# Early score tiles placed by the count of each row half, and first query rows and keys fetched earlier, in a fused attention and MLP kernel

## The chip, the cores and the metric

The kernel runs on one core of one Trainium2 chip. The time is device time in microseconds; the kernel before took 1616.31 us, the median of three runs (1616.12 to 1617.63). A core has a matrix engine (TensorE, called PE in the profile, with its weight loads as PEld), VectorE (DVE), ScalarE (ACT), GpSimd (POOL) and SyncE (SP), which here only issues DMA transfers. Matmul results go to PSUM, eight banks of 128 x 512 float32.

## The reference

For x of 2048 tokens by 512, a layer norm feeds an attention block of 32 heads of 16 and an MLP of width 1376; the output is x plus their product.

```python
xn = _layernorm(x, axis=-1)
s = _A_ref(xn, A_wqkv, A_wo)          # softmax(q k^T / 4) v, 32 heads, then @ wo
g = _silu(_B_ref(xn, B_w1, B_b1, B_w2, B_b2))   # gelu_tanh(xn @ w1 + b1) @ w2 + b2
return x + s * g
```

## The kernel before

**Stages.** The first stage (lines 382 to 520) normalizes x, transposes it and keeps it as a high part and a low part; every product of the projections is then three matmuls (high by high, high by low, low by high). It also computes the query and key rows of the first two head groups (`q_first`, four calls, one for each chunk of 512 tokens) and four of the value tiles (`v_tile`). Query and key rows are stored to device memory (`evac`, lines 373 and 374, queued on SP) and fetched again in another layout by `load_qs` (queries), `load_k` (keys) and `k_ones`.

The second stage, called the early stage here, runs the list `plan` (line 303): twelve value tiles in three `quad`s, 34 pairs of tiles of the MLP's first layer or of the remaining query and key rows (`half`, two for each pair), and 88 parts of the MLP's second layer (`down`). All its matmuls have a contraction of 64 rows. Two row tiles of the array are used, half 0 (rows 0 to 63) and half 1 (rows 64 to 127); `run` emits one matmul for each in turn, and one round of it is called a step here. There are 12 x (12 + 68) + 88 x 6 = 1488 steps, so 1488 of these matmuls (line 564) on each half.

The third stage is the attention itself: score tiles transposed, exponentials on ACT, products with the values (lines 712, 714, 778), then the output projection.

**The score tiles.** Before the exponentials can be taken, the maximum over keys of each query row and head has to be known. A score tile computes 128 query rows by 512 keys of one head with one matmul (line 180, contraction 48: high and low parts in three groups of 16 rows) and reduces it to two maxima on DVE (line 186). There are 32 units u (8 head groups by 4 chunks of queries) of 64 tiles. 4 x LEAD = 576 tiles, the units 0 to 8, are done in the early stage, between the other matmuls; the rest in the attention stage. Score tiles are done in turn on half 0 and half 1 (`made`), and their PSUM tiles come in turn from two banks, `ps_a` and `ps_b` (`s_ring`). When a unit is done, its maxima are negated and split (`s_end0`), which also asks for the query rows of the unit after next, and later transposed on PE (`s_end1`, line 260), copied by ACT (line 266) and stored.

**What places them.** `run` calls `fill(a)` ahead of each matmul of half a. `prog["n"]` counts the steps. `fill` emits a score tile if fewer have been made than `due`, which grows in a straight line from step FILL0 = 84 to step SLOTS = 1470, and if it is that half's turn; a transposition that has become ready takes the place of a tile.

**Waits between the halves.** A PSUM bank that was written from one half may be written from the other only after that; `mm` then has the matmul wait for a small ACT instruction (`mark`, line 577, tile `junk`), unless three later score tiles say that the earlier matmul is done (`taken`).

**Queues and errands.** SP issues its transfers in the order of the program. In the early stage `half` takes one entry each time from the list `errands`: the fetches of query rows (`ask_qs`) and of the keys of the next groups (`ask_k`: one for the rows of ones, six for the keys). The first query rows and keys are fetched at lines 716 to 718, behind the stores of the last `q_first`; the last call of the first stage, `v_tile(NCH - 1)`, stands at line 520. `load_k` fetches six pieces of 16 rows: three for each half.

**Order within a unit.** `at_of` turns a tile's number into a block of query rows and a chunk of keys; all units but u = 12 take the key chunks fastest.

Of the kernel before, what the change touches and what calls it, by code (L numbers as in the profile page):

```python
# [17 lines left out]
S = 2048  # L18
# [5 lines left out]
CH = 512  # L24
NCH = S // CH
# [7 lines left out]
LEAD = 144  # L33
NW = 10
EARLY = 4
DONE = 492
FILL0 = 84
HB = 4
W2B = 2
ORDER = {0: "TTTTV", 3: "TXSTTSTYV"}  # L40
# [1 line left out]
KB = 3  # L42
# [5 lines left out]
def fused(ctx: ExitStack, tc: tile.TileContext, x, wqk, wv, wo, w1, b1, w2, b2, out):  # L48
# [27 lines left out]
    def mm3(ps, lhs, rhs, first, last, then=None):  # L76
        n = 0
        for a, b in ((0, 0), (0, 1), (1, 0)):
            nc.tensor.matmul(ps, lhs[a], rhs[b], start=first and n == 0, stop=last and n == 2)  # L79
            n += 1  # L80
            if then:
                then()
# [14 lines left out]
    def rows(src, g, which, a, c0, n):  # L97
        r0 = g * P + 64 * which + DH * a
        return src[r0:r0 + 48, c0:c0 + n].rearrange("(p d) s -> d p s", d=DH)[:, 0:3:2, :]

    def load_k(g, pieces=range(6), eng=nc.sync, c0=0, n=S):
        both = kws[g % KB]
        for i in pieces:
            a, b = divmod(i, 3)
            r, cs = slice(64 * a + DH * b, 64 * a + DH * b + DH), slice(c0, c0 + n)
            src = rows((qk_h, qk_h, qk_l)[b], g, 1, a, c0, n)
            if both is not None:
                eng.dma_start(both[r, :, cs].bitcast(F32), src)
            else:
                for p in range(2):  # L110
                    eng.dma_start(kts[g % KB][p][r, cs].bitcast(F32), src[:, p])
# [16 lines left out]
    def q_rows(qs, u, sides=range(2)):  # L128
        g, c = divmod(u, NCH)
        for a in sides:  # L130
            for b, src in enumerate((qk_h, qk_l, qk_h)):
                r = 64 * a + DH * b
                nc.sync.dma_start(qs[r:r + DH].bitcast(F32), rows(src, g, 0, a, c * CH, CH))

    def load_qs(u, sides=range(2)):
        if u < NU:
            QS[u] = qzs[u % 2] if u < LEAD // 16 else qss[0][:, u % 2]
            q_rows(QS[u], u, sides)

    def ask_qs(u):  # L140
        for a in range(2):
            errands.append((load_qs, u, (a,)))

    def load_qt(u):
        QT[u] = qts[u % 2]
        q_rows(QT[u], u)
# [7 lines left out]
    made = [0, 0]  # L154
    done = {u: 0 for u in range(NU)}
    later, ended, errands, sent = [], [], [], set()

    def tick():
        for e in later:
            e[0] -= 1  # L160
# [7 lines left out]

    def at_of(job):
        u, st, p = job  # L170
        return divmod(st, NCH) if u != NCH * KB else divmod(st, NCH)[::-1]

    def s_mm(ps, job, a, c0, k0, w):
        u, st, p = job
# [20 lines left out]
    def s_whole(job, a):  # L195
        ps = s_tile()[0]
        s_mm(ps, job, a, 0, 0, CH)
        s_max(ps, job, a, slice(0, 2))

    def s_one(a):  # L200
        made[a] += 1
        s_whole(heads[made[a] - 1], a)
# [53 lines left out]
    prog = {}  # L256
# [23 lines left out]
    def w_new(src, bufs, tag):  # L280
        raw = wk.tile([P, CH], F32, name=tag, bufs=bufs)
        nc.sync.dma_start(raw, src)
        return raw
# [8 lines left out]
    VQ = 3  # L292
    first = [[("v", t // NCH, t % NCH) for t in range(i, i + 4)] for i in range(NT - 4 * VQ, NT, 4)]
    qs = [(2, 0), (2, 2)] + [(g, 0) for g in range(3, NG)] + [(g, 2) for g in range(3, NG)]
    nu, pairs = len(ms) // 2, []
# [8 lines left out]
    for j in range(len(pairs)):  # L304
        for h in range(2):
# [4 lines left out]
            due = next((i for i in range(j, len(pairs)) if is_m[i]), len(pairs))  # L310
# [4 lines left out]
            n = 2 if nd < len(parts) and parts[nd][2] and ready - nd > room else 1  # L315
            n = max(n, need - 2 * (left - 1))
# [27 lines left out]
    def w2_load(i):  # L344
        if i < len(ms):
            W2[ms[i][1:]] = w_new(w2[ms[i][2]], 2, "raw2")
# [31 lines left out]
    def v_out(t, pv):  # L378
        dst = vsb[:, t, :H * VW].rearrange("p (h w) -> p h w", w=VW)[:, :, :DH]
        nc.scalar.activation(dst, pv.rearrange("p (h w) -> p h w", w=DH), AF.Copy)  # L380

    with ExitStack() as s1:
# [4 lines left out]
        def a_tile(shape):  # L387
            banks[0] += 1
            i = banks[0] % 6
            if i < 3:  # L390
                return (ps_a, ps_b, ps_x)[i].tile(list(shape), F32, name="ps")
            return ps_t.tile(list(shape), F32, name="pst")
# [42 lines left out]
        def v_tile(t):  # L435
            pv = a_tile((P, D))
            c, ts = t // NCH, slice(t % NCH * P, t % NCH * P + P)
            for k in range(KT):
                mm3(pv, (xh[c][:, k, ts], xl[c][:, k, ts]), (wv_h[:, k], wv_l[:, k]), k == 0, k == KT - 1)
            v_out(t, pv)  # L440

        def q_first(c):
            pq = {}
            for g in range(2):
                ps = pq["q", g, c] = a_tile((P, CH))
                for k in range(KT):
                    ks = slice(k * P, (k + 1) * P)
                    mm3(ps, (W1[g][0][:, ks], W1[g][1][:, ks]), (xh[c][:, k], xl[c][:, k]), k == 0, k == KT - 1)
            evac(list(pq), pq)
# [58 lines left out]
        for c in range(1, NCH):  # L508
            for t in range(NCH * c, NCH * c + NCH):
                turn(t)  # L510
            if c < NCH - 1:
                ln(NCH * c + NCH, NCH)
            else:
                nc.scalar.activation(warm[:, 1:], warm[:, :1], AF.Gelu_apprx_tanh)
                w1_load(0)
                w2_load(0)
                w2_load(1)
            v_tile(c - 1)
            q_first(c)
        v_tile(NCH - 1)  # L520

    keep_r = ctx.enter_context(tc.tile_pool(name="keep_r", bufs=1, side="right"))
    qring = ctx.enter_context(tc.tile_pool(name="qring", bufs=2, side="right"))
# [6 lines left out]
    for i in range(2):  # L530
        qzs.append(qzp.tile([P, 2, CH], F32R, name=f"qz{i}"))

    prog.update(n=0, pe=0, seen=0)
    writer = {}
    s_when = []
    ndown = sum(1 for e in plan if e[0] == "down")
    SLOTS = 12 * (4 * VQ + 2 * len(pairs)) + 6 * ndown - 18

    def fill(a):
        due = 4 * LEAD * (prog["n"] - FILL0) // (SLOTS - FILL0)  # L540
        if sum(made) < min(due, 4 * LEAD) and (made[0] <= made[1]) == (a == 0):
            taken()
            if later and later[0][0] <= 0:
                u = later.pop(0)[1]
                s_end1(u)
                s_end2(u)
                return
            s_one(a)
            tick()

    def taken():
# [5 lines left out]
    def mm(a, key, ps, lhs, rhs, first, last):  # L557
        r = slice(64 * a, 64 * a + 64)
        token = None
        if not first and writer[key][0] != a and writer[key][1] > prog["seen"]:  # L560
            if not tokens or tokens[-1][0] < writer[key][1]:
                mark()
            prog["seen"], token = next(x for x in tokens if x[0] >= writer[key][1])
        i = nc.tensor.matmul(ps, lhs[r], rhs[r], start=first, stop=last).ins  # L564
        if token is not None:
            tc.add_manual_dep(i, token, SYNC, reason="other row tile")
        prog["pe"] += 1
        latest[0] = (prog["pe"], i.name)
        writer[key] = (a, prog["pe"])

# [104 lines left out]
    def quad(n):  # L675
        us = first[n]
        for u, b in zip(us, BANKS[n]):
            pool, name = {"x": (ps_x, "ps"), "m": (ps_m, "ps"), "v": (ps_v, "pv"), "t": (ps_t, "pst")}[b]
            PH[u] = pool.tile([P, CH], F32, name=name)
        for i in range(4):  # L680
            hooks = {6: [mark]} if i in (1, 2) else {}
            if n == VQ - 2 and i in (0, 2):
                hooks[3] = [lambda: w1_split(0) if i == 0 else w1_load(1)]
            run((terms(us[i], 0, i < 2), terms(us[(i + 2) % 4], 1, i < 2)), hooks)
            if i >= 2:
                for u in (us[i - 2], us[i]):
                    v_out(u[1] * NCH + u[2], PH.pop(u))
# [25 lines left out]
                         QT[u][r, p, :], start=True, stop=True)  # L713
        nc.scalar.activation(PT[u, k][:, 2 * p + a, :], ps, AF.Exp, scale=SCALE)  # L714

    load_k(0)
    load_qs(0)
    k_ones(kts[0])
    for n, e in enumerate(plan):
        if e[0] == "half":  # L720
            half(*e[1:])
        elif e[0] == "first":
            quad(e[1])
        else:
            if e[1] == parts[-2]:
                nc.scalar.activation(mhw, ident_r[:1, :1].bitcast(F32), AF.Exp)
            if e[1] == parts[-1]:
                for i in range(EARLY):
                    t_one(0, 0, i // 2, i % 2)
            down(*e[1])  # L730
        if e == ("first", VQ - 1):
            w2_split(0)
            w2_load(2)
            ask_qs(1)
            ask_k(1)
        if e[0] == "half" and pairs[e[1]][0] == ("q", NG - 1, 0) and e[2] == 1:
            kts.append([slot(p, (P, S), F32R) for p in range(2)])
            kws.append(None)
            qss.append(slot(2, (P, 2, 2, CH), F32R))
            ask_k(2)  # L740
        if n == len(plan) - 8:
            load_qt(0)
            load_mh(0)
# [172 lines left out]
    for t in range(NW):  # L916
        n = DONE + 2 * t
# [6 lines left out]
    for i, t in enumerate(late):  # L924
        n = L - 2 * len(late) - 1 + 2 * i
# [84 lines left out]
```

## Time and profile before

| | us |
|---|---|
| median of three runs | 1616.31 |
| profiled execution, its own time | 1617.43 |
| its span, first to last instruction | 1615.6 |
| PE busy | 1603.2 (99%) |
| DVE busy | 1388.1 (86%) |
| ACT busy | 1259.4 (78%) |
| POOL busy | 379.1 (23%) |
| early stage, first to last matmul of line 564 | 53.71 to 491.94 |

The span does not hold what lies ahead of the first instruction and behind the last; that is why the profiled execution's own time is 1.8 us more. A row of a timeline gives the start and the length in us, the engine, the line, the operation with output and inputs, the shape and how many instructions were merged into the row. A row of a stretch of time gives the length of the stretch, then busy time and instructions for each engine, the granted clock (1.00 is full speed), the busy share of the DMA engines and the GB/s they moved. The mean granted clock of the core was 0.999.

### The profile page before, as it was taken

The page shows a single profiled execution, that of the slowest core. Times are in us where ns is not written, and L with a number is a line of the kernel's source. Part 1 is how long each engine was busy: PE and PEld are TensorE (multiplying, and loading weights), DVE is VectorE, ACT ScalarE, POOL GpSimd, SP SyncE. Part 2 cuts the span into 40 slices and gives each one's busy share as a digit, 9 for nine tenths or more (in the row PEclk, how much of TensorE's full clock was granted, in tenths as well). Part 3 has the DMA queues.
Part 4 walks back from the last instruction along what each step waited for, and adds up shares of the span by engine and source line. Part 5 has one row for each costly group of instructions (what it writes and reads, how often), then busy time and mean ns, then how long its engine had stood idle before and what let it go on. Part 6 is the DMA issues. An engine that isn't in the chain of part 4 may idle for free.

```text
span 1615.6 us, 32457 instructions
## 1 busy us (share of the span) xinstructions
PE 1603.2 (99%) x12146; PEld 926.5 (57%) x12146; DVE 1388.1 (86%) x2267; ACT 1259.4 (78%) x2524; POOL 379.1 (23%) x398
## 2 busy tenths in 40 slices
PE   8999999999999999999999999999999999999998
PEld 7899999989995444444444444444444444444445
DVE  7299999989998999999999999999999999999733
ACT  4324333333338999999999999999999999999984
POOL 4235565655641001001100200000010000000144
PEclk9999999999999999999999999999999999999999
DMA  6615343453422113111511311231041111110152
GB/s 202 143 55 156 116 135 96 128 153 113 135 81 74 30 40 67 32 35 27 85 35 32 67 31 40 45 55 28 21 78 29 32 28 32 39 29 22 58 197 92
DMA packets 76223, 116.93 MB, mean 72 GB/s; under 512 B 24965, under 2 KB 26245, under 8 KB 74697
## 3 DMA queue, kind: packets, MB, share of 16 engines
q1 hardware_dynamic: 72604, 102.42, 23.3%
q0 software_dynamic: 3264, 12.35, 3.9%
q8 instruction: 96, 1.57, 0.4%
q14 instruction: 63, 0.51, 0.1%
q10 hardware_dynamic: 196, 0.07, 0.0%
HBM read 84.35 MB, written 25.97 MB: 68 GB/s over the span
## 4 chain that ended last, share of the span: by engine, by line
PE 97%; DVE 1%; ACT 0%; DMA 0%; issue 0%; SPq 0%; DVEq 0%; ACTq 0%
PE pv L778 32%; PE ps L180 18%; PE pst L712 15%; PE ps L564 13%; PE pst L564 7%; PE ps L712 5%; PE ps L79 3%; PE pv L564 2%; PE pst L79 1%; DVE slot L74 0%; DMA xt<-in_x 0%; ACT hh L367 0%; PE pst L260 0%; DVE st L408 0%; DVE xn L422 0%
## 5 line engine op out<-in xcount | busy, mean ns | idle before, releaser
L186 DVE TENSOR_REDUCE mx<-ps 128x2 f32<-128x512 f32 x2048 | 1307.8, 686 | 155.0 <-PE ps L180 97.6
L714 ACT ACTIVATE slot<-pst 128x512 f32<-128x512 f32 x1533 | 836.1, 614 | 14.5 <-PE pst L712 4.3
L778 PE MATMUL pv<-slot,vsb 128*32 128x512 f32 x4096 | 545.3, 605 | 0.0
L180 PE MATMUL ps<-kt,slot 48*128 48x512 f32 (+1 forms) x1364 | 393.3, 376 | 0.0
L712 PE MATMUL pst<-qt,kt 50*128 50x512 f32 x1149 | 378.7, 430 | 0.4 <-DVE gt L645 0.3
L714 ACT ACTIVATE slot<-ps 128x512 f32<-128x512 f32 x515 | 315.7, 614 | 14.0 <-PE pst L712 9.5
L712 PEld LDWEIGHTS pst<-qt,kt 50*128 50x128 f32 x1149 | 183.1, 184 | 248.3 <-ACT slot L714 245.1
L564 PE MATMUL ps<-slot,w1h 64*128 64x512 f32 x1088 | 232.9, 393 | 0.4 <-ACT junk L577 0.4
L180 PEld LDWEIGHTS ps<-kt,slot 48*128 48x128 f32 x1364 | 211.3, 184 | 34.6 <-DVE mx L186 23.4
L180 PE MATMUL ps<-kt,qz 48*128 48x512 f32 x512 | 218.8, 429 | 0.9 <-ACT mh L266 0.9
L180 PE MATMUL ps<-slot,slot 48*128 48x512 f32 (+1 forms) x598 | 172.5, 376 | 0.7 <-DVE mx L186 0.7
L564 PEld LDWEIGHTS ps<-slot,w1h 64*128 64x128 f32 x1088 | 159.9, 185 | 9.3 <-ACT junk L577 1.9
L712 PE MATMUL ps<-qt,kt 50*128 50x512 f32 x387 | 163.1, 423 | 0.0
L564 PE MATMUL ps<-slot,w1l 64*128 64x512 f32 x544 | 158.9, 393 | 0.0
L778 PEld LDWEIGHTS pv<-slot,vsb 128*32 128x32 f32 x4096 | 80.6, 108 | 119.5 <-issue 111.7
L368 POOL TENSOR_TENSOR hl<-hg,hh 128x512 fp32r<-128x512 f32 x76 | 96.7, 1294 | 133.6 <-ACT hh L367 83.6
L577 ACT ACTIVATE junk<-ident_r 1x1 f32<-1x1 f32 x92 | 18.1, 196 | 136.9 <-PE pst L564 133.0
L712 PE MATMUL pst<-qt,slot 50*128 50x512 f32 x384 | 119.7, 424 | 0.0
L712 PEld LDWEIGHTS ps<-qt,kt 50*128 50x128 f32 x387 | 71.2, 184 | 70.3 <-ACT slot L714 57.4
L712 PEld LDWEIGHTS pst<-qt,slot 50*128 50x128 f32 x384 | 61.5, 184 | 71.9 <-ACT slot L714 71.6
L180 PEld LDWEIGHTS ps<-slot,slot 48*128 48x128 f32 x598 | 92.6, 184 | 16.9 <-DVE mx L186 13.3
L244 POOL CAST nmh<-nm 128x16 fp32r<-128x16 f32 x32 | 6.3, 197 | 409.3 <-PE pst L712 258.0
(150 smaller groups left out, 1760.3 us busy)
## 6 DMA issues: line engine op xcount, KB each, us to landing
raw<-in_w SPq DMA_DIRECT2D x88, 256.0 KB
qk_h<-hh SPq DMA_DIRECT2D x32, 256.0 KB
qk_l<-hl SPq DMA_DIRECT2D x32, 256.0 KB
qt<-qk_h SPq DMA_DIRECT2D x128, 64.0 KB
slot<-qk_h SPq DMA_DIRECT2D x92, 64.0 KB
xt<-in_x SPq DMA_DIRECT2D x16, 256.0 KB
g_d<-gt POOLq DMA_DIRECT2D x16, 256.0 KB, 3.6
qt<-qk_l SPq DMA_DIRECT2D x64, 64.0 KB
```

The lines of the kernel that those rows point to most:

```text
L79: nc.tensor.matmul(ps, lhs[a], rhs[b], start=first and n == 0, stop=last and n == 2)
L180: return nc.tensor.matmul(ps[:, c0:c0 + w], QS[u][r, p, qi * P:(qi + 1) * P], kts[u // NCH % KB][p][r, k0:k0 + w], start=True, stop=True).ins
L186: nc.vector.tensor_reduce(MX[u][:, 2 * p:2 * p + 2, qi, ki][:, heads, parts], ps.rearrange("p (n c) -> p n c", c=HC), axis=AX.X, op=OP.max)
L244: nc.gpsimd.tensor_copy(hl[:, 0], nm)
L368: nc.gpsimd.tensor_sub(hl, raw, hh.bitcast(F32))
L564: i = nc.tensor.matmul(ps, lhs[r], rhs[r], start=first, stop=last).ins
L577: i = nc.scalar.activation(junk[:, :1], ident_r[:1, :1].bitcast(F32), AF.Copy).ins
L712: nc.tensor.matmul(ps, kts[g % KB][p][r, k * P:(k + 1) * P], QT[u][r, p, :], start=True, stop=True)
L714: nc.scalar.activation(PT[u, k][:, 2 * p + a, :], ps, AF.Exp, scale=SCALE)
L778: nc.tensor.matmul(PV[u][32 * j:32 * j + 32, :], vsb[:, k, h:h + 32], PT[u, k][:, j, :], start=(k == 0), stop=(k == NT - 1))
```

## The change

Score tiles are placed by a count of each half's own matmuls, `row[a]`, which takes in the score tiles. Tile number m goes to half a as soon as `row[a]` reaches FILL0 + m x ROWS / 576, with FILL0 = 38 and ROWS = 960 + 528 - 10 + 288 - 16 - 38 = 1712; `put` moves the due counts by two for each transposition that was emitted. The number of tiles stays 576.

The first stage's last part (`v_tile(NCH - 2)`, the last `q_first`, `v_tile(NCH - 1)`) is emitted after the pools of the next stage are opened; the query rows of unit 0 and the keys of its group, without the last 512 columns, are fetched ahead of it, and the last 512 columns behind it. The units 0, 12 and 24 now take the query blocks fastest, so that unit 0 begins with the first chunk of keys. Query rows asked for go to the front of the errands, and those of unit 1 are asked for after the first quad instead of the third.

```diff
-FILL0 = 84
+FILL0 = 38
@@
     def ask_qs(u):
-        for a in range(2):
-            errands.append((load_qs, u, (a,)))
+        errands[:0] = [(load_qs, u, (a,)) for a in range(2)]
@@
     def at_of(job):
         u, st, p = job
-        return divmod(st, NCH) if u != NCH * KB else divmod(st, NCH)[::-1]
+        return divmod(st, NCH) if u % (NCH * KB) else divmod(st, NCH)[::-1]
@@
                 w1_load(0)
                 w2_load(0)
                 w2_load(1)
+                break
             v_tile(c - 1)
             q_first(c)
-        v_tile(NCH - 1)
@@
         qzs.append(qzp.tile([P, 2, CH], F32R, name=f"qz{i}"))
 
+    load_qs(0)
+    load_k(0, c0=0, n=S - CH)
+    v_tile(NCH - 2)
+    q_first(NCH - 1)
+    v_tile(NCH - 1)
+    load_k(0, c0=S - CH, n=CH)
+
     prog.update(n=0, pe=0, seen=0)
     writer = {}
-    s_when = []
+    s_when, put, row = [], [0], [0, 0]
     ndown = sum(1 for e in plan if e[0] == "down")
-    SLOTS = 12 * (4 * VQ + 2 * len(pairs)) + 6 * ndown - 18
+    ROWS = 12 * (4 * VQ + 2 * len(pairs)) + 6 * ndown - 10 + 2 * LEAD - 2 * (LEAD // 16 - 1) - FILL0
 
     def fill(a):
-        due = 4 * LEAD * (prog["n"] - FILL0) // (SLOTS - FILL0)
-        if sum(made) < min(due, 4 * LEAD) and (made[0] <= made[1]) == (a == 0):
+        due = FILL0 + put[0] + sum(made) * ROWS // (4 * LEAD)
+        if sum(made) < 4 * LEAD and row[a] >= due and (made[0] <= made[1]) == (a == 0):
             taken()
             if later and later[0][0] <= 0:
+                put[0] += 2
                 u = later.pop(0)[1]
                 s_end1(u)
                 s_end2(u)
                 return
             s_one(a)
+            row[a] += 1
             tick()
@@
         prog["pe"] += 1
+        row[a] += 1
         latest[0] = (prog["pe"], i.name)
@@
-    load_k(0)
-    load_qs(0)
     k_ones(kts[0])
     for n, e in enumerate(plan):
@@
             quad(e[1])
+            if e[1] == 0:
+                ask_qs(1)
@@
             w2_load(2)
-            ask_qs(1)
             ask_k(1)
```

## The prediction

> **What bounds the kernel now.** I read the page's busy times and the chain of waits first, then the early stage by lines in one long stretch.
>
> ```profile
> PE 1603.2 (99%) x12146; PEld 926.5 (57%) x12146; DVE 1388.1 (86%) x2267; ACT 1259.4 (78%) x2524; POOL 379.1 (23%) x398
> PE 97%; DVE 1%; ACT 0%; DMA 0%; issue 0%; SPq 0%; DVEq 0%; ACTq 0%
> ...
> 64.97 2.75 PE ps L564 x24
> ...
> 73.50:487.00 413.50, 411.41 (x2768) 364.14 (x2766) 1.00 0.39 114
> ...
> 73.50:487.00 413.50, 245.51 (x575) 105.09 (x575) 1.00 0.39 114
> ```
>
> The third row is from the chain, the fourth and fifth are one stretch with the instructions of L564 and of L180 alone. PE sets the end, so what the early stage loses is lost at the end. Each matmul there uses one half of the array's rows, and two run at once: 24 matmuls in 2.75 us are 12 on each half, 0.229 us a place (I call a half's n-th matmul its place n). In the stretch with score tiles 2768 + 575 = 3343 matmuls took 413.5 us, or 0.247 us a place. PE shows as busy all the same, because one matmul's record is 0.39 us long and covers pauses. So pauses must be sought between starts. The stretch holds 575 score tiles, one every 0.719 us.
>
> The timeline of PE shows where the stage begins and ends, and how the halves run:
>
> ```profile
> 53.71 0.49 PE L564 MATMUL pst<-kt,slot 64*128 64x512 f32 x1
> ...
> 73.50 0.39 PE L180 MATMUL ps<-kt,qz 48*128 48x512 f32 x1
> 73.52 0.84 PE L564 MATMUL pst<-kt,slot 64*128 64x512 f32 x4
> 73.97 0.39 PE L180 MATMUL ps<-kt,qz 48*128 48x512 f32 x1
> ...
> 487.00 0.50 PE L180 MATMUL ps<-slot,qz 48*128 48x512 f32 x1
> ...
> 491.94 0.39 PE L564 MATMUL pst<-w2h,hl 64*128 64x512 f32 x1
> ```
>
> From the rule in fill, worked by hand: the first score tile stands at step 87, place 86 of half 0 (86 x 0.229 = 19.7 us after 53.71: 73.4, seen 73.50), the second at step 89, place 88 of half 1. In the order of the code five matmuls lie between them, three on half 0; yet they start 0.47 us apart, two places. So each half runs down its own list, and places, not steps, are time. In steps the tiles are 2 or 3 apart; a tile on half 1 follows by that many places, the next on half 0 by one more, its own half holding one more score tile. Counted out over 575 gaps: 270 gaps of three places, 172 of two, 117 of four, 16 others. Stretches of it, score tiles alone:
>
> ```profile
> 91.69 0.39 PE L180 MATMUL ps<-kt,qz 48*128 48x512 f32 x1
> ...
> 95.11 0.44 PE L180 MATMUL ps<-kt,qz 48*128 48x512 f32 x1
> ...
> 100.17 0.40 PE L180 MATMUL ps<-kt,qz 48*128 48x512 f32 x1
> 100.68 0.50 PE L180 MATMUL ps<-kt,qz 48*128 48x512 f32 x1
> 101.56 0.40 PE L180 MATMUL ps<-kt,qz 48*128 48x512 f32 x1
> 102.20 0.40 PE L180 MATMUL ps<-kt,qz 48*128 48x512 f32 x1
> 102.95 0.46 PE L180 MATMUL ps<-kt,qz 48*128 48x512 f32 x1
> 103.59 0.43 PE L180 MATMUL ps<-kt,qz 48*128 48x512 f32 x1
> ...
> 107.23 0.40 PE L180 MATMUL ps<-kt,qz 48*128 48x512 f32 x1
> ```
>
> Compare ends (start plus length). From 91.69 to 95.11, and from 100.17 to 103.59, five gaps of three places: 3.47 and 3.45 us for 15 places, 0.231 and 0.230 us each. From 103.59 to 107.23, gaps of 2, 4, 2, 4, 2: 3.61 us for 14 places, 0.258. So threes cost nearly what matmuls alone cost, and the uneven set loses 3.61 - 14 x 0.232 = 0.36 us.
>
> Why: two PSUM banks, each freed by a reduction on DVE.
>
> ```profile
> 100.60 0.69 DVE L186 TENSOR_REDUCE mx<-ps 128x2 f32<-128x512 f32 x1
> ...
> 101.21 0.69 DVE L186 TENSOR_REDUCE mx<-ps 128x2 f32<-128x512 f32 x1
> ...
> 102.78 0.68 DVE L186 TENSOR_REDUCE mx<-ps 128x2 f32<-128x512 f32 x1
> ...
> 100.67 0.18 PEld L180 LDWEIGHTS ps<-kt,qz 48*128 48x128 f32 x1
> ...
> 101.96 0.18 PEld L180 LDWEIGHTS ps<-kt,qz 48*128 48x128 f32 x1
> ```
>
> The load at 100.67 leads to the matmul ending at 101.18 (0.51 us); its reduction starts at 101.21 (0.03), ends at 101.90 (0.69), and the next load into that bank starts at 101.96 (0.06). At best a bank therefore serves a tile every 0.51 + 0.03 + 0.69 + 0.06 = 1.29 us. This particular bank took 102.78 - 101.21 = 1.57 us, because its load went ahead of a matmul still running and its reduction waited behind the other bank's. Reductions start no closer than 0.61 us (100.60, 101.21). A gap of two places (0.46 us) undercuts that, and two gaps of five places in all (1.16 us) undercut the bank; six places (1.39 us) do not.
>
> **The change part by part, and the sum.** No matmul, reduction or transfer of bytes is added or removed; 576 tiles stay in the stage.
>
> Spacing. The new rule counts places: 1712/576 = 2.972 per tile from place 38 on. Worked out the same way: 551 gaps of three places, 16 of two, 8 of five (where a transposition of the maxima stands between); first tile at place 38, last at 1763 (before: 86 and 1756, of 1776). Now 1725 places lie in the stretch instead of 1670.
>
> Other pauses, which both kernels have:
>
> ```profile
> 126.87 0.50 PE L180 MATMUL ps<-kt,qz 48*128 48x512 f32 x1
> ...
> 129.68 0.49 PE L180 MATMUL ps<-kt,qz 48*128 48x512 f32 x1
> ...
> 80.44 0.50 PE L564 MATMUL ps<-slot,w1h 64*128 64x512 f32 x1 [0.36 <-ACT junk L577]
> ...
> 360.10 0.50 PE L180 MATMUL ps<-kt,qz 48*128 48x512 f32 x1 [0.86 <-ACT mh L266]
> ```
>
> Between the first two rows stand ten places and one transposition: 2.80 - 2.32 = 0.48 us, eight times is 3.8. The two single waits are 0.36 + 0.86 = 1.2. The account of before: 1670 x 0.232 = 387.4, plus 3.8, 1.2 and some 58 uneven sets (575 gaps, ten to a cycle) x 0.36 = 20.9, is 413.3, against 413.5 measured.
>
> The new stage: 38 x 0.229 = 8.7; 1725 x 0.232 = 400.2; transpositions 3.8; single waits 1.2; sixteen two-place gaps between threes, which before does not show. Their price is at least 1.29 - 1.16 = 0.13 us and at most the 0.36 of a whole uneven set; I take 0.36, the nearer row being the whole set: 5.8. Tail: the 20 places behind the last tile took 491.94 - 487.00 + 0.23 = 5.2; seven fewer make it 3.6. With 0.5 for the first fetch, below, that is 423.8. Before: 19.8 + 413.5 + 5.2 = 438.5. The stage gets **14.7 us shorter**. The ends of the place price (0.229 to 0.2335) move this by -5.2 and +2.6, those of the gap by -3.7 and 0.
>
> First rows fetched earlier. Six loads of query rows and six of keys (three quarters of the columns) pass, on SP's queue, the four last stores and then go out; six small loads of the last quarter of the keys are new, 12 issues become 18.
>
> ```profile
> 45.08 1.92 SPq L282 DMA_DIRECT2D raw<-in_w  x4
> ...
> 55.43 0.79 SPq L108 DMA_DIRECT2D kt<-qk_h  x2
> ...
> 70.96 0.84 SPq L282 DMA_DIRECT2D raw<-in_w  x2
> ...
> 58.00:62.00 4.00, 1.00 1.03 164
> 62.00:66.00 4.00, 1.00 1.05 157
> ...
> 50.00:52.00 2.00, 1.00 0.43 162
> ```
>
> SP is free at 47.0 instead of 55.4, and the engines work off the weights by about 51 (busy share 0.43 in 50 to 52). The query rows (0.39 MB) and three quarters of the keys (1.18 MB) at 160 GB/s, the rate of the two stretches that carried keys, take 9.8 us: an estimate of 61. The new first tile stands at 53.71 + 8.7 = 62.4, and its partner on the other half, which needs the last of these pieces, at 63.1. The cover is 2 us, so the price is 0 to 2 us; I take 0.5, as completion comes after the last byte. Before, there was ample cover: the first tile stood at 73.5. The four stores behind these loads may go out some us late; behind them wait the last quarter (first read at tile 48, 53.71 + (38 + 48 x 2.97) x 0.23 = 95), the rows of ones and the weights of 70.96, whose place in the program does not move. If SP came late to those by more than a few us, ACT's split and the matmuls on it would wait the difference.
>
> Fetches of later query rows go to the front of the list of errands and the first of them is asked a hundred steps earlier: steps 105 and 111 for a tile at step 197. The keys of group 1 still finish at step 339, needed at 677; those of group 2 at 1089 instead of 1053, needed at 1318. Cost nothing; PE would stand still if one were late. The changed order of tiles for u = 24 touches the same tiles. Waits that hand a PSUM bank between halves fall from 12 to 9 by the same count, too few to enter.
>
> The profiled execution took 1617.43 with a span of 1615.6; the median of the runs is 1616.31. The attention stage follows unchanged, so 14.7 less is 1602.7 profiled and **1601.6 us** for the median.
>
> **The rivals.** (1) *The banks go on setting the pace.* If a tile still takes 0.719 us, the stretch stays at 413.5 but starts 11.1 us earlier and ends closer to the end: 8.7 + 413.5 + 3.6 + 0.5 = 426.3, or 12.2 less, 1604.1. For it: loads start right behind the freeing reduction. Against: the 0.230 of threes. The Trainium skill, page "TensorEngine Tiling (Array Packing)", section "PSUM Bottleneck", leans this way: tiling speeds up TensorE but not the evacuation of PSUM; the 1.29 us of a bank against 1.39 demanded says that here there is just room.
>
> (2) *The first tile waits for all keys*, as if the tile were one unit to its readers. Then the four stores and the last quarter come first: 3.0 MB at 160 GB/s from 51 is 69.8, 7.4 us after 62.4; 0.5 was in the sum: 1608.5. Against: the keys come in pieces with ranges of columns.
>
> (3) *The halves do not run apart.* If matmuls started strictly in the order of the code, seven matmuls would lie between tiles one way and three the other, four places and two. Each second reduction would wait 0.61 - 0.46 = 0.15 us, a bank would take 1.29 + 0.15 = 1.44 against 1.39 in demand: 287 pairs x 0.05 = 14 us, nearly all of the gain, 1616. Against: the 0.47 us above. The Trainium skill, page "TensorE: Matmul & The Clock Gate", section "The mechanism", does state strict program order for matmuls; this trace, with 0.47 us where that needs 0.69, disagrees for the two halves.
>
> (4) *Slower: the tiles lock in pairs.* If half 1 lags half 0 by more than 0.09 us, even threes come closer than 0.61 us in one direction, the late bank takes the 1.57 us seen above each time, and nothing breaks the beat since no gap of four comes to reset it. Then a tile costs 0.785, the stretch 575 x 0.785 + 5.0 = 456.4, the stage 469.2, 30.7 longer: 1647. It decides from (438.5 - 8.7 - 3.6 - 0.5)/575 = 0.740 us a tile on. For it: the ends in the second run of threes come 0.61 to 0.64 and 0.78 to 0.81 apart in turn. Against: their sum stays at 0.230 a place.
>
> **How the numbers follow.** My forecast holds with 0.62, rival 1 with 0.17, 2 with 0.07, 3 with 0.04, 4 with 0.08; 0.02 is left for something else that is slower. The range 1594 to 1609 has the ends of the two prices (1601.6 - 8.9 = 1592.7 if both fall out low together, so 1594), rival 1, and rival 2 at its top; 3, 4 and the rest lie outside. About 0.2%, 3.2 us, is what a measurement here can tell from no change. Faster: 0.62 + 0.17 + 0.07 = 0.86; within: 0.04; slower: 0.10.
>
> **What would show it.** First score tile at 62.4 (62 to 64; 70 for rival 2); the mean of 575 gaps 0.70 (0.72 rival 1, over 0.74 rival 4), with gaps of about 0.70 each way if 3 is wrong; loads no longer always 0.06 behind a reduction; the last matmul of L564 at 477; from there to the end as long as before. I am wrong if that last stage grows, or if the early gaps come out as before with no earlier first tile.

## The result, and the profile after

The changed kernel took 1607.73 us in the median (1606.84 to 1608.24, four runs) against 1616.21 (1615.77 to 1617.63, four runs) of the kernel before: a ratio of 0.9945, 95% interval 0.9928 to 0.9963. That is 8.5 us less, where 14.7 were forecast. The line numbers of the new kernel are one less up to the new code and 8 or 9 more behind it: score matmul L179 (was L180), reduction L185 (L186), the early stage's other matmuls L572 (L564).

The page's busy times and chain by engine:

```profile
PE 1594.5 (99%) x12146; PEld 915.4 (57%) x12146; DVE 1384.3 (86%) x2267; ACT 1261.6 (79%) x2525; POOL 377.6 (24%) x398
...
PE 98%; DVE 1%; DMA 0%; issue 0%; ACT 0%; SPq 0%; DVEq 0%; ACTq 0%
```

PE sets the end as before, with the same number of matmuls and 8.7 us less busy time, pauses between starts included. Where in the stage that lies shows in three stretches: from the first L572 matmul to the first score tile, from there to the last score tile, and to the last L572 matmul. The rows are those of score instructions alone (L179).

```profile
53.43:62.24 8.81, 0.00 (x1) 0.18 (x1) 1.00 0.97 134
62.24:479.62 417.38, 241.14 (x575) 105.13 (x575) 1.00 0.40 118
479.62:482.88 3.26, 0.40 (x1) 0.09 (x1) 1.00 0.42 155
```

| | before | after | difference |
|---|---|---|---|
| first other matmul to first score tile | 19.8 | 8.8 | -11.0 |
| first to last score tile | 413.5 | 417.4 | +3.9 |
| last score tile to last other matmul | 4.9 | 3.3 | -1.7 |
| from there to the end of the span | 1123.7 | 1123.6 | -0.1 |

All of the gain comes from the earlier start and the later last tile. The stretch with tiles did not keep its pace of 0.719 us a tile: 417.38/575 = 0.726. The attention stage has not moved by more than 0.1 us.

The start in PE's timeline, and SP's queue ahead of it:

```profile
62.24 0.39 PE L179 MATMUL ps<-kt,qz 48*128 48x512 f32 x1
62.25 1.07 PE L572 MATMUL pst<-kt,slot 64*128 64x512 f32 x5
63.62 0.47 PE L179 MATMUL ps<-kt,qz 48*128 48x512 f32 x1 [0.30 <-issue]
```

```profile
46.69 0.33 SPq L133 DMA_DIRECT2D qz<-qk_h  x1
...
55.08 0.41 SPq L108 DMA_DIRECT2D kt<-qk_l  x1
55.61 0.86 SPq L372 DMA_DIRECT2D qk_h<-hh  x1
...
70.30 0.83 SPq L281 DMA_DIRECT2D raw<-in_w  x2
```

The loads begin at 46.7; the last of the first three quarters of the keys is issued at 55.1, the first of the last stores at 55.6, and the next weights still at 70.3 (before: 70.96). The first tile starts at 62.24. Its partner on half 1, two places on, starts 1.38 us behind it; in e2 below, where the rows have long been there, it starts 0.47 behind. So the price of the fetch is 0.9 us at this tile.

Now a piece of the steady part. All gaps here are of three places.

```profile
91.09 0.39 PE L179 MATMUL ps<-kt,qz 48*128 48x512 f32 x1
91.22 0.39 PE L572 MATMUL pst<-kt,slot 64*128 64x512 f32 x1
...
91.69 0.39 PE L179 MATMUL ps<-kt,qz 48*128 48x512 f32 x1
...
92.48 0.45 PE L179 MATMUL ps<-kt,qz 48*128 48x512 f32 x1
92.62 0.39 PE L572 MATMUL pst<-kt,slot 64*128 64x512 f32 x1
...
93.09 0.43 PE L179 MATMUL ps<-kt,qz 48*128 48x512 f32 x1
93.94 0.39 PE L179 MATMUL ps<-kt,qz 48*128 48x512 f32 x1
94.53 0.40 PE L179 MATMUL ps<-kt,qz 48*128 48x512 f32 x1
```

```profile
91.68 0.69 DVE L185 TENSOR_REDUCE mx<-ps 128x2 f32<-128x512 f32 x1 [0.28 <-PE pst L572]
...
92.29 0.68 DVE L185 TENSOR_REDUCE mx<-ps 128x2 f32<-128x512 f32 x1
...
93.09 0.69 DVE L185 TENSOR_REDUCE mx<-ps 128x2 f32<-128x512 f32 x1
```

The tile of half 1 that starts at 91.09 ends at 91.48. Its reduction could follow 0.04 us behind, as others do; DVE is idle. It starts at 91.68, and the profile names an L572 matmul as what released it. That is the one of 91.22, which ends at 91.61, 0.07 before. In the code it stands ahead of the score tile; by the order of the code it is on half 0, whose list at that point holds one score tile more, so it runs a place later. The same at 92.48 (ends 92.93; the matmul of 92.62 ends at 93.01; the reduction starts at 93.09). The tile of half 0 that follows then finds DVE busy: from 91.68 to 92.29 is 0.61, the least distance of two reductions. So half 1's tile is late by a wait and half 0's by a queue, both hold their banks longer, and tiles end 0.60 and 0.80 to 0.85 us apart in turn: ends 91.48, 92.08, 92.93, 93.52, 94.33, 94.93. Over the whole stretch 258 of 287 reductions of half 1 start this way, on average 0.17 us behind their own tile, and 279 of 287 of half 0 start on DVE's heels, 0.18 us behind theirs. From one reduction to the next but one, the cycle of a bank, the median is 1.42 us; before, it was 1.40.

The list of waits shows the same, cut to reductions and to the stretch with tiles, with us, times and the longest; the first fence is the kernel before, the second the changed one:

```profile
DVE mx L186 <- PE ps L564: 8.2, 30, 0.7
DVE mx L186 <- PE pst L564: 4.4, 17, 0.3
...
DVE mx L186 <- PE pv L564: 2.1, 8, 0.3
```

```profile
DVE mx L185 <- PE ps L572: 8.4, 41, 0.7
DVE mx L185 <- PE pst L572: 5.1, 23, 0.7
DVE mx L185 <- PE pv L572: 1.8, 9, 0.3
```

A reduction takes its input from a score matmul alone, yet 55 times before and 73 times after it was another matmul that let an idle DVE go on. The list counts only idle times above 0.15 us, so these are fewer than the 258 above.

### The profile page after: what moved, and what is told of

It reads as the page before. It is cut to its first block, busy times and chain, and to the rows that moved or that the text cites. A ratio compares the mean times of both kernels' runs of the same rounds, so it can differ in the third digit from the quotient of the medians.

```text
span 1606.5 us, 32467 instructions
## 1 busy us (share of the span) xinstructions
PE 1594.5 (99%) x12146; PEld 915.4 (57%) x12146; DVE 1384.3 (86%) x2267; ACT 1261.6 (79%) x2525; POOL 377.6 (24%) x398
## 3 DMA queue, kind: packets, MB, share of 16 engines
q8 instruction: 96, 1.57, 0.4%
## 4 chain that ended last, share of the span: by engine, by line
PE 98%; DVE 1%; DMA 0%; issue 0%; ACT 0%; SPq 0%; DVEq 0%; ACTq 0%
PE pv L786 32%; PE ps L179 18%; PE pst L721 16%; PE ps L572 12%; PE pst L572 7%; PE ps L721 5%; PE ps L79 4%; PE pv L572 2%; PE pst L79 1%; DVE slot L74 0%; DMA xt<-in_x 0%; DVE st L407 0%; PE pst L259 0%; PE ps L259 0%; DVE xn L421 0%
## 5 line engine op out<-in xcount | busy, mean ns | idle before, releaser
L185 DVE TENSOR_REDUCE mx<-ps 128x2 f32<-128x512 f32 x2048 | 1300.2, 685 | 155.2 <-PE ps L179 86.1
L179 PE MATMUL ps<-kt,slot 48*128 48x512 f32 (+1 forms) x1364 | 393.1, 376 | 0.0
L179 PEld LDWEIGHTS ps<-kt,slot 48*128 48x128 f32 x1364 | 211.4, 184 | 34.5 <-DVE mx L185 25.6
L572 PE MATMUL ps<-slot,w1h 64*128 64x512 f32 x1088 | 220.1, 394 | 0.4 <-ACT junk L586 0.4
L179 PE MATMUL ps<-kt,qz 48*128 48x512 f32 x512 | 214.9, 420 | 0.3 <-issue 0.3
L179 PE MATMUL ps<-slot,slot 48*128 48x512 f32 (+1 forms) x598 | 172.4, 376 | 0.7 <-DVE mx L185 0.7
L572 PEld LDWEIGHTS ps<-slot,w1h 64*128 64x128 f32 x1088 | 152.5, 185 | 8.0 <-ACT junk L586 1.8
L572 PE MATMUL ps<-slot,w1l 64*128 64x512 f32 x544 | 143.0, 393 | 0.0
L179 PEld LDWEIGHTS ps<-kt,qz 48*128 48x128 f32 x512 | 93.7, 183 | 17.4 <-DMA kt<-qk_h 0.7
```

What stands on the lines that cost most here:

```text
L179: return nc.tensor.matmul(ps[:, c0:c0 + w], QS[u][r, p, qi * P:(qi + 1) * P], kts[u // NCH % KB][p][r, k0:k0 + w], start=True, stop=True).ins
L185: nc.vector.tensor_reduce(MX[u][:, 2 * p:2 * p + 2, qi, ki][:, heads, parts], ps.rearrange("p (n c) -> p n c", c=HC), axis=AX.X, op=OP.max)
```

## The experiments

Theory A, from these rows: a reduction waits for a count of finished matmuls in the order of the code. Rival B: the bank's pace comes from loads, reductions and PE alone. Rival C: PE itself is slower per place when score tiles are among its matmuls, whatever the banks do. All ratios are against the kernel before, run on the same chip.

**e1, tiles emitted first.** In the step, both halves' `fill` come ahead of both matmuls.

```diff
             for a in range(2):
                 fill(a)
+            for a in range(2):
                 mm(a, *two[a])
```

> The changed kernel, but in each step both halves' score tiles are emitted ahead of both other matmuls; places as in the changed kernel (threes). In its trace 258 of 287 reductions of half 1 start 0.07 us behind the end of an L572 matmul that ends later than their own score tile. Theory A: a reduction waits for a count of finished matmuls in the order of the code, so a tile of half 1, emitted behind its step's matmul of half 0, counts as done only a place later. Then A expects here: reductions of half 1 about 0.04 us behind their own tile, a score tile every 0.71 instead of 0.726 us, early stage 423 instead of 429.5, time 1599 to 1603. Rival B: the bank pace of 0.726 comes from loads, reductions and PE alone: 1607 to 1609, nothing changes. Rival C: PE itself needs 0.242 us a place when score tiles are among the matmuls: also 1607 to 1609.

Measured 1600.36 us, ratio 0.9900 (0.9885 to 0.9915). The stretch, and reductions released by another matmul (all such rows of the list of waits):

```profile
61.36:470.98 409.62, 229.22 (x576) 105.33 (x575) 1.00 0.42 120
```

```profile
DVE mx L185 <- PE ps L572: 0.8, 1, 0.8
DVE mx L185 <- PE pst L572: 0.8, 1, 0.8
```

Two releases of that kind instead of 73, reductions of half 1 on average 0.05 us behind their tile instead of 0.16 over all of them, 409.62/575 = 0.712 us a tile: A, and the size it named. B and C fall for the difference between the two kernels.

The trace also records when semaphores rise, the flags by which one engine waits for another. Score matmuls and L572 matmuls raise the same one, and all 576 reductions wait for it. In the changed kernel it first rises 0.014 us (median) behind the end of a score tile of half 0, but 0.11 us behind the end of one of half 1; in e1 it is 0.014 for both. So it is the signal of a finished matmul that comes late, and turning the order round takes the delay away.

A piece of e1's trace, score matmuls of PE, a load and two reductions:

```profile
92.52 0.39 PE L179 MATMUL ps<-kt,qz 48*128 48x512 f32 x1
...
93.92 0.40 PE L179 MATMUL ps<-kt,qz 48*128 48x512 f32 x1
...
92.30 0.18 PEld L179 LDWEIGHTS ps<-kt,qz 48*128 48x128 f32 x1
...
92.95 0.69 DVE L185 TENSOR_REDUCE mx<-ps 128x2 f32<-128x512 f32 x1
...
94.36 0.69 DVE L185 TENSOR_REDUCE mx<-ps 128x2 f32<-128x512 f32 x1
```

From the load at 92.30 to the matmul's end at 92.91 are 0.61 us here, as the matmul starts 0.22 behind its load; then 0.04 to the reduction, 0.69, and 0.05 to the next load: 1.39 us a cycle, with PE never pausing (92.95 to 94.36 is 1.41). Six places are 6 x 0.232 = 1.39 as well, so these rows don't tell whether the bank or PE's list sets the cycle; e5 does.

**e2, first tile at place 86.** The changed kernel with one constant.

```diff
-FILL0 = 38
+FILL0 = 86
```

> The changed kernel with its first score tile at place 86, where the kernel before had it, and the same last place: 1677 places for 576 tiles instead of 1725. Theory A and rival B (banks set the pace, 0.726 us a tile): the stretch stays at 417, the stage grows by the 11 us of the later start, time 1617 to 1620, the whole gain is gone. Rival C (PE needs 0.242 us a place): the stretch shrinks to 406, time 1606 to 1609.

Measured 1619.51 us, ratio 1.0017 (1.0007 to 1.0026): the gain is gone, with a little more.

```profile
73.30:491.17 417.87, 247.99 (x576) 104.90 (x575) 1.00 0.39 113
```

3% fewer places for the same number of tiles, and the stretch is as long as the changed kernel's, 0.727 us a tile: while the late signals hold the banks, the banks set the pace, not PE. Rival C falls altogether. It also gives the new order of the tiles without the earlier start: by itself it is no gain.

**e3, the old steps with the new start.** Tiles every 2.5 steps, from the same place 38; FILL0 is 36 and SLOTS, a new line, 1476.

```diff
-        due = FILL0 + put[0] + sum(made) * ROWS // (4 * LEAD)
-        if sum(made) < 4 * LEAD and row[a] >= due and (made[0] <= made[1]) == (a == 0):
+        due = 4 * LEAD * (prog["n"] - FILL0) // (SLOTS - FILL0)
+        if sum(made) < min(due, 4 * LEAD) and (made[0] <= made[1]) == (a == 0):
```

> The changed kernel, its early fetches and its start at place 38, but the score tiles placed by steps, one every 2.5: gaps of two places (half 0 to half 1) and four places in turn. Theory A: the end that a tile of half 1 counts by is a place later, so these are even in effect; a tile every 0.70 us, the stage 417 to 422, time 1595 to 1601, faster than the changed kernel. The prediction's view (even places are best, two places undercut the 0.61 us of DVE) and rival B: 1608 to 1615. Rival C: 1607 to 1609.

Measured 1600.27 us, ratio 0.9899 (0.9884 to 0.9914), the stretch 409.9 us. Gaps of two and four places in turn beat gaps of three by 7 us, as A expected, though a tile takes 0.713 us and not 0.70. The wait is not gone: 164 of 288 reductions of half 1 and 116 of half 0 are still released by another matmul. But the cycle's median is 1.40 us instead of 1.42, so here it costs next to nothing. A's reason, that half 1's tile is early by the place by which the count is late, is not shown by this.

**e4, both edits.**

> Both edits at once: tiles every 2.5 steps (two and four places in turn) and both halves' tiles emitted first. Theory A: now the tiles count as done where they end, so two and four places are uneven in effect; reductions of half 1 wait for DVE, time 1606 to 1615, worse than either edit alone. If the edits helped for reasons of their own, both together would be at least as fast as the better one. Rivals B and C: 1607 to 1609.

Measured 1600.45 us, ratio 0.9898 (0.9883 to 0.9912), the stretch 409.9. A's expectation was missed. It held that two and four places must be uneven in effect once the count is no longer late. In the trace 133 reductions of half 1 do start on DVE's heels, 0.11 us late on average; but tiles end 0.63 and 0.78 us apart in the median, not 0.46 and 0.93. The halves shift against each other until DVE's 0.61 is kept, and the sum of two gaps stays six places. So evenness of the places is worth nothing here; what counts is six places for two tiles, and no wait that makes the bank's cycle longer than that.

**e5, e1 with the first tile at place 86.** The edits of e1 and e2 together.

> The kernel of e1 (both halves' tiles emitted first) with its first tile at place 86 and the same last place: 1677 places, 2.89 a tile. It asks what limits e1, where a tile cost 0.712 us. If PE does (e1's stretch less 5.0 for transpositions and single waits is 404.6 for 1725 places, 0.2346 a place), the stretch becomes 1677 x 0.2346 + 5.0 = 398 and the time stays at 1600 to 1602. If the banks do (a cycle of 1.40 us for two tiles, which e1 and the kernel before share), the stretch stays at 410 and the later start costs 11 us: 1610 to 1613.

Measured 1607.54 us, ratio 0.9943 (0.9925 to 0.9961), between the two expectations.

```profile
73.27:478.75 405.48, 237.58 (x576) 105.30 (x575) 1.00 0.40 116
```

The stretch is 405.5, not 398 and not 410, because both limits are at work. Counted out from the rule as in the prediction, two tiles that follow each other in one bank are five places apart 123 times and six places 435 times (transpositions left out); in e1 it is 30 and 528 times. From the reduction of one to that of the next, the median is 1.28 us for five places and 1.40 for six, in e5 and in e1 alike. Three reductions of one bank, two score matmuls and a load:

```profile
96.89 0.69 DVE L185 TENSOR_REDUCE mx<-ps 128x2 f32<-128x512 f32 x1
...
98.28 0.69 DVE L185 TENSOR_REDUCE mx<-ps 128x2 f32<-128x512 f32 x1
...
99.56 0.69 DVE L185 TENSOR_REDUCE mx<-ps 128x2 f32<-128x512 f32 x1
...
97.85 0.39 PE L179 MATMUL ps<-kt,qz 48*128 48x512 f32 x1
...
99.03 0.49 PE L179 MATMUL ps<-kt,qz 48*128 48x512 f32 x1
...
99.03 0.18 PEld L179 LDWEIGHTS ps<-kt,qz 48*128 48x128 f32 x1
```

From 96.89 to 98.28 are six places and 1.39 us, from 98.28 to 99.56 five places and 1.28. In the second the load starts 0.06 behind the end of the reduction, the matmul ends 0.49 later at 99.52, and the next reduction starts 0.04 behind: the bank's least cycle of the prediction (1.29). Five places at 0.233 would be 1.17, so there the bank holds PE up; six places take 1.40, more than the bank needs, so there PE's own list is what is left to set the pace, at 0.233 a place.

**e6, the fetch where it was.** The changed kernel with `load_k(0)` and `load_qs(0)` back behind the last `v_tile`, whole, ahead of `k_ones`.

```diff
-    load_qs(0)
-    load_k(0, c0=0, n=S - CH)
@@
-    load_k(0, c0=S - CH, n=CH)
@@
+    load_k(0)
+    load_qs(0)
     k_ones(kts[0])
```

> The changed kernel with the first query rows and keys fetched as before, behind the last stores, keys first; its first tile still stands at place 38, 62.2 us. In the kernel before the last of these loads was issued at 66.4, and SP saw the keys land at about 61 to 69. If the earlier fetch is what makes the earlier start possible, the first tiles wait until about 69, PE with them, and the time grows by 6 to 8 us to 1614 to 1616. If something else hides it (the loads faster when nothing else runs, or the first tile not in need of the late pieces), 1607 to 1610.

Measured 1618.76 us, ratio 1.0014 (1.0004 to 1.0023). PE's timeline at the first tile, due at 62.4:

```profile
61.78 0.85 PE L569 MATMUL pst<-kt,slot 64*128 64x512 f32 x5
71.34 0.76 PE L179 MATMUL ps<-kt,qz 48*128 48x512 f32 x1 [8.71 <-DMA kt<-ones_d]
```

PE stands still for 8.7 us. The name behind the wait is not the cause, as a score tile reads no row of ones. In the semaphore records the score tile's load waits until 71.04, and the first of these two loads of query rows finishes landing at 71.01:

```profile
61.48 2.04 SPq L133 DMA_DIRECT2D qz<-qk_h  x2
```

Behind the pause the granted clock is low for some 4 us:

```profile
71.00:75.00 4.00, 3.66 (x18) 3.16 (x20) 2.08 (x3) 0.00 (x0) 0.00 (x0) 0.51 0.05 12
75.00:79.00 4.00, 4.00 (x37) 3.63 (x35) 3.11 (x5) 2.12 (x4) 1.02 (x1) 1.00 0.00 0
```

Half as many matmuls fit in (18 instead of 37). The stretch as a whole is 418.4 us, 1.1 more than in the changed kernel. The direction was expected, the size was 3 to 5 us more: I had put the landing at 69, by the keys and not by the query rows behind them. The early fetch is worth 11 us by the medians; without it the earlier start brings nothing.

**e7, the kernel before with tiles emitted first.** The edit of e1 on the old kernel, nothing else.

> The kernel before with one edit, both halves' tiles emitted ahead of both other matmuls of the step; placed by steps from 84 as before. In its trace 214 of 574 reductions were released by another matmul than their own. If the wait for a matmul in the order of the code is what held it at 0.719 us a tile, the stretch of 1670 places falls to 1670 x 0.2346 + 5.0 = 397 and the time to 1599 to 1603, without the change. If the banks' own cycle of 1.40 us held it, or its gaps of two places (172 of them) then wait for DVE, 1612 to 1618.

Measured 1607.19 us, ratio 0.9940 (0.9922 to 0.9957), again between: the stretch is 404.1 us instead of 413.5. So the count's wait cost the old kernel 9.4 us too. What remains is as in e5: 116 cycles of five places with a median of 1.28 us and 442 of six with 1.40. One added line without the change brings as much as the change.

e1, e3 and e4 are each 7 us faster than the changed kernel; among themselves they don't differ by what these runs can tell.

## Why the prediction was right and where it was not

**Start and tail: right.** First tile forecast at 62.4, seen 62.24; head 8.7 against 8.8; the tail 3.6 against 3.3 to the start of the last matmul, 3.5 with the 0.23 that the sum counted; the fetch 0.5 against 0.9, in the bounds of 0 to 2. The first tile's partner was put at 63.1, three places behind; by the rule it stands two behind. e6 shows that the fetch is what permits the start.

**The stretch: the step that failed.** The sum had "1725 x 0.232 = 400.2; transpositions 3.8; single waits 1.2", plus 5.8 for two-place gaps and 0.5 for the fetch, 411.5 in all. It took 417.4. The step that failed is the price of a place. It was read from five gaps of three places, and compared with the five uneven gaps that follow. The tiles of those, between the rows that the prediction shows, are:

```profile
104.33 0.49 PE L180 MATMUL ps<-kt,qz 48*128 48x512 f32 x1
105.02 0.40 PE L180 MATMUL ps<-kt,qz 48*128 48x512 f32 x1
105.83 0.39 PE L180 MATMUL ps<-kt,qz 48*128 48x512 f32 x1
106.42 0.42 PE L180 MATMUL ps<-kt,qz 48*128 48x512 f32 x1
```

In both sets the ends come at short and long distances in turn. In the threes (ends 100.57 to 104.02) they are 0.61, 0.78, 0.64, 0.81 and 0.61 apart, three short and two long; in the uneven set (104.02 to 107.63) 0.80, 0.60, 0.80, 0.62 and 0.79, two short and three long. Over four gaps, two of each kind, both have 12 places and take the same: 2.84 us in the threes, 2.82 in the uneven set. In the whole trace of the kernel before, the medians over four such gaps are 2.85 and 2.81. So threes cost 0.238 a place, above the prediction's upper end of 0.2335. With 0.238 the term is 410.6, and with 3.8, 1.2 and 0.5, and nothing for two-place gaps, the sum is 416.1. The sum had 10.4 too little for the places and 5.8 priced by a loss that uneven sets don't have; that the two partly cancelled was luck.

What makes threes dear is the wait that e1 removes. The prediction charged the late reduction at 102.78 to the other bank's, which is so; but the other bank's was late itself, and its row was not weighed:

```profile
102.18 0.69 DVE L186 TENSOR_REDUCE mx<-ps 128x2 f32<-128x512 f32 x1 [0.27 <-PE pv L564]
```

Its tile had ended at 101.96 and DVE was idle. In the changed kernel, where nearly all gaps are threes, that wait comes at nearly every tile of half 1, and a cycle of six places takes 1.42 us; in e1 it takes 1.40, or 0.233 a place. What the sum lacked is this wait, 417.4 - 409.6 = 7.8 us. Without it the sum's way holds: 1725 places at 0.233 (from e1's own trace) are 401.9, with 3.8, 1.2, 0.7 for the fetch in e1 and the prediction's lower price of 0.13 for each of the sixteen two-place gaps 409.7, against 409.6 measured. The bank's least cycle of 1.29, from which that price comes, was read rightly (e5).

**Evenness: wrong.** The "0.36 us of a whole uneven set" was read as the cost of uneven gaps, from the five gaps above. e3 and e4 run at the same 0.713 us a tile with two and four places in turn throughout.

**The rivals.** Rival 1, the banks go on setting the pace, is what happened in the changed kernel, where 0.726 us a tile does not answer to fewer places (e2: 0.727). The Trainium skill, page "TensorEngine Tiling (Array Packing)", section "PSUM Bottleneck", says that tiling does not speed up the evacuation of PSUM. This kernel agrees, with the late signal as part of the evacuation; without it most cycles go at PE's pace (e5). The price of 1604.1 missed by 3.6 us, as the pace did not stay at 0.719: 575 x 0.007 = 4.0. Rival 2 did not come: the first tile ran at 62.24, before the last quarter was issued at 64.8. Rival 3 is half true. The Trainium skill, page "TensorE: Matmul & The Clock Gate", section "The mechanism", states that matmuls start and end in the order of the program. Here neither holds between the halves (the L572 matmul of 91.22 ends behind the score tile of 91.09 that stands after it in the code), but what waits for them is let go in the order of the code. Rival 4 came in a mild form: tiles do go in pairs, 0.60 and 0.83 us apart, with a cycle of 1.42 and not 1.57. Pairs alone cost nothing: in e1 they are 0.61 and 0.79 apart, at 1.40.

## What to carry to other kernels

When matmuls of two row tiles run apart, emit the one that others wait for ahead of its neighbours on the other tile; a consumer can be held by a matmul it has no use for, and one added line that turns the order round gave 7 us on the changed kernel and 9.6 on the one before. A ring of two PSUM banks has a least cycle of load, matmul, reduction and two hand-overs; a producer that asks for less than that only moves the pause. Measure such a ring over whole cycles, an even number of tiles: tiles come in pairs, and five gaps made two sets that cost the same look 0.36 us apart here. When a stage is bound by such a ring, start it earlier and check what it waits for first: here that was the fetch.

## What the runs showed of the hardware that was not expected

A reduction whose own matmul had ended started about 0.07 us behind the end of another matmul, on the other row tile and earlier in the code: 258 of 287 in the changed kernel, 1 of 287 once the order was turned round. The signal that the reductions wait for rose 0.11 us (median) behind the end of a score tile of half 1 there, and 0.014 once the order was turned round. The value that each reduction waits for is not recorded; that it is a count of matmuls in the order of the code is inferred from these times and from e1 and e7.

A weight load followed by its matmul ended 0.49 to 0.51 us after the load's start where the matmul started at once, and 0.61 where it started 0.22 behind the load. That a matmul of the same half was still running in the second case is likely, but no row names the half.

Two halves with uneven lists did not keep the distance that the lists give (two and four places, 0.46 and 0.93 us) but slid to 0.63 and 0.78, at no cost in sum.

After PE had stood still for 8.7 us in e6, its granted clock was 0.51 for 4 us and then 1.00 again.
